# Three id arrays, routing steps and gathers at other places, and T3 kept in PSUM in a chain of attention and two expert layers

## The chip, the cores and the metric

One core of one Trainium2 chip runs one program. The metric is the device time in microseconds (us): the median of 3 runs of the kernel before is 2043.76 us (2043.2 to 2044.96).

## The reference, cut to what matters

```python
# 1. linear attention, B=4 H=8 S=576 D=64, features 2*128
phi = lambda x: concat[exp(p - m), exp(-(p - m))],  p = x @ w_phi, m = max|p|
x = (phi(q) @ (phi(k).T @ v)) / (phi(q) @ sum(phi(k)) + 1e-6)     # -> x[2304, 512]
# 2. soft expert layer, 8 experts, F=1024: every token through every expert
P = exp(x @ w_gate - max); 8 times: rows / sum, columns / sum, * N/E
x = sum_e P[:, e] * (relu(x @ w1[e]) @ w2[e])
# 3. top-1 expert layer: each token through the one expert with the largest cosine
e = argmax(norm(x) @ norm(emb).T / tau);  g = softmax(...)[e]
out = g * (relu(x @ w1[e]) @ w2[e])
```

## The kernel before, in words

All products are made of fp32r parts: each operand is split into a high part (ScalarE cast) and a rest (one subtraction), and three matmuls are summed for one product (L429 to L431).

**First expert layer.** There are 16 half-experts, the groups `n`, and three token batches of 768, so 48 steps `h`. A step is a seven-product Strassen scheme in both layers of the expert: 28 products of six 384-column matmuls. Steps of groups 2 to 14 run through `layers()`; those of groups 0, 1 and 15 run through `p1_group()` and `p2_plain()` with 14 and 16 products. A product is a **tick**. Work beside the products is put on a list by (step, tick): `at_tick()` and `ops_at()` write it, `run_at()` emits it after that product. Each engine then does its instructions in the order in which they were emitted. Ticks of 40 and more in the tables mean the next step.

In `layers()` the hidden halves are B11, B22, T3, T1, T2, B21, T4 in that order. `high()` is a ScalarE cast (L474), `rest()` the subtraction (L477): on GpSimd (POOL in the profile) for B11, B22, T3, T2 and T4, on VectorE (DVE) for T1 and B21. `A.copy(vc, b0)` (L519) empties a PSUM pair that product S4 then writes. T3 is put into an SBUF tile `rc`. `m1c` (L498) is copied into the tile `ra`, which also holds T4's source for its rest.

The last step of each group (`h % NB == NB - 1`) is the **weight-making step**: beside the products it makes the eight split weight pieces of W1 for the next group, and at its end and in the following step those of W2. A piece is a ScalarE cast (L348) and a GpSimd subtraction (L349); four of them first need a GpSimd combination (L354).

**Routing.** Tokens' rows go to DRAM (`x2d`); per tile of 128 tokens an indirect DMA of GpSimd (`route_i`, L960) scatters (token number, gate) pairs into DRAM arrays `ids[k]`, at the slot of the token's expert. There are RB = 6 arrays, one for each tile of a batch of six, and a slot's value is the sum over the arrays. Routing of batches 0 and 6 (tiles) runs in the last two steps (`tail`, by ticks), that of the last batch at the start of `second()`. `route_a` transposes a tile through the PSUM bank "B", of which there is one.

**Second expert layer.** `second()` runs 22 blocks of 128 slots. For each: `load_ids(i)` reads three registers (`value_load`) and issues RB small DMAs on SyncE's queue (L1060); `gather(i)` sums them with a matmul (L1068), VectorE copies token numbers and gates out of PSUM (L1070, L1072), and an indirect DMA of GpSimd fetches the rows (L1074). `tx` transposes and splits them, `p1`, `relu`, `th_`, `p2` are the two layers. `w1_next` and `w2_this` split the weights of the next block's first and this block's second layer on ScalarE and VectorE (L1107, L1108); behind each split a conditional DMA on SyncE (`wcond`, L1079) loads the piece for the block after. Loop order of the kernel before: `load_ids(i+3)`, `p1(i)`, `w1_next(i)`, `relu(i)`, `tx(i+1)`, `w2_this(i)`, `p2(i-1)`, `gather(i+3)`, `th_(i)`. Block 6 is the first whose ids depend on the last batch; `load_ids(6)` stands behind `w2_this(3)`.

Of the kernel before, what the change touches and what calls it, by code (L numbers as in the profile page):

```python
# [23 lines left out]
DM = H * D  # L24
# [5 lines left out]
TH = TB // 2  # L30
NB = NT // TB
TPB = TB // P
RB = 6
NBLK = NT // P + E
REG = NT
NSLOT = 19456
# [8 lines left out]
def build(tc, a, out):  # L45
# [424 lines left out]
    def hraw(tag):  # L470
        return live["h3"].tile([P, 2, TH], F32, tag="r" + tag, name="r" + tag)
# [4 lines left out]
    def rest(nm, src, eng):  # L476
        eng.tensor_tensor(out=hb[nm][:, 1], in0=src, in1=f32(hb[nm][:, 0]), op=ALU.subtract)  # L477
# [6 lines left out]
    def layers(h, n, bi):  # L484
        odd = h % 2
        qx, qz = (0, 3) if odd else (3, 0)

        def tt(out, x, y, op=ALU.subtract):
            V.tensor_tensor(out=out, in0=x, in1=y, op=op)  # L489

        def read(q_, ps, op=ALU.add):
            z = acc(bi)[:, q_]
            V.tensor_tensor(out=z, in0=z, in1=ps, op=op)  # L493

        b0 = pair(qz)
# [24 lines left out]
        b2 = pair(2)  # L520
        yield from twin(b2, 1, "S3", xs["T3"], True)
        tt(b1, b2, vc, ALU.add)
        r22 = hraw("d")
        gate(r22, 1, b1)
        high("B22", r22)
        for i, _ in enumerate(twin(b0, 1, "S4", xs["B22"], False)):
            if i == 0:
                rest("B22", r22, G)
            yield
        gate(b0, 1, b0)  # L530
        t3 = hraw("c")
        tt(t3, r22, b0)
        high("T3", t3)
        tt(b0, b0, r11)
        high("T1", b0)
        for i, _ in enumerate(twin(b2, 1, "A22", xs["T4"], False)):
            if i == 0:
                rest("T3", t3, G)
            yield
        tt(b2, b2, u2c, ALU.add)  # L540
        rest("T1", b0, V)
        tt(r22, r22, b0)
        high("T2", r22)
        gate(b2, 0, b2)
        high("B21", b2)
        X = pair(qx)
        for i, _ in enumerate(twin(X, 2, "A11", hx["B11"], True)):
            if i == 0:
                rest("T2", r22, G)
            yield  # L550
        Y = pair(1)
        yield from twin(Y, 2, "S4", hx["B22"], True)
        read(1, Y, ALU.subtract)
        read(0, X)
        rest("B21", b2, V)
        Z = pair(qz)
        yield from twin(Z, 2, "S1", hx["T1"], True)
        t4 = hraw("a")
        tt(t4, r22, b2)
        high("T4", t4)  # L560
        read(1, Z)
        for i, _ in enumerate(twin(Y, 2, "S3", hx["T3"], False)):
            if i == 0:
                rest("T4", t4, G)
            yield
        read(3, Y)
        yield from twin(X, 2, "S2", hx["T2"], False)
# [303 lines left out]
    def x2c(t0, i, k):  # L871
        return acc(t0 // TPB)[:, 2 * (k // 2) + i // 3, k % 2, (i % 3) * P:(i % 3 + 1) * P]

    def route_a(t0, i):
        r = batch(t0)
        m = TPB // len(r["pieces"])
        row = r["pieces"][i // m][:, i % m]
        ps = psum("B", [P, DM])
        for k in range(KD):
            T.transpose(ps[:, k * P:(k + 1) * P], x2c(t0, i, k), ident)  # L880
        A.activation(out=row, in_=ps, func=AF.Square, accum_out=r["ss"][:, i:i + 1])
        A.copy(row, ps)
# [74 lines left out]

    def route_i(t0, i):
        si = rt[t0]["si"]
        G.indirect_dma_start(out=ids[i], out_offset=bass.IndirectOffsetOnAxis(si[:, i:i + 1], 0), in_=pay[:, t0 + i, :], in_offset=None)  # L960

    meta = c0.tile([1, 3, NBLK], I32, name="meta")
    ebx = c0.tile([1, NBLK + 1], F32, name="ebx")
# [72 lines left out]

    def route_steps(t0, ta, tl, **rest):
        fns = dict(p=route_p, b=route_b, o=route_o, c=route_c, s=route_s, d=route_d, w=route_w)
        ev = [(k, partial(route_l, t0, i)) for i, k in enumerate(tl)] + [(k, partial(route_a, t0, i)) for i, k in enumerate(ta)]
        ev += [(k, partial(fns[nm], t0)) for nm, k in rest.items() if nm != "i"]  # L1040
        return ev + [(k, partial(route_i, t0, i)) for i, k in enumerate(rest["i"])]

# [189 lines left out]
    for h, (n, bi) in enumerate(HS):  # L1232
# [11 lines left out]
        if h % NB == NB - 1 and n + 1 < NGR:  # L1244
            o1, o2 = wops(1, n + 1), wops(2, n + 1, SL1 if n == 0 else SL15 if n == NGR - 2 else {})
            if mixed(n):
                ops_at(h - 1, ((4, "S1r"), (8, "S3r")), o1)
                ops_at(h, ((2, "A11"), (3, "S2r"), (7, "S2"), (8, "A12"), (9, "S4r"), (10, "S1"), (12, "S3"), (14, "S4"), (16, "A22 load")), o1)
            else:
                ops_at(h, ((8, "A11"), (9, "S1r"), (10, "S3r"), (11, "S2r"), (13, "A12"), (14, "S4r"), (16, "S2"), (18, "S1"), (20, "S3"), (22, "S4"), (24, "A22 load")), o1)  # L1250
            if n == 0:
                ops_at(h, ((24, "A11"), (25, "A12"), (26, "A21"), (28, "A22 load")), o2)
            elif n == 1:
                ops_at(h, ((22, "S1r"), (23, "S3r"), (24, "A12"), (26, "A22"), (28, "S3"), (40, "A11"), (41, "S2r"), (42, "S4r"), (44, "S1"), (46, "S4"), (49, "S2 load")), o2)
            elif n == NGR - 2:
                ops_at(h, ((18, "A11"), (24, "A21"), (28, "A12"), (40, "A22 load")), o2)
            else:
                ops_at(h, ((18, "A11"), (20, "S1r"), (21, "S3r"), (25, "S2r"), (40, "A12"), (41, "S4r"), (43, "S1"), (45, "A22"), (46, "S4"), (49, "S3"), (51, "S2 load")), o2)
        if h >= 2 * NB - 1 and h + 1 < NH:
            at_tick(h, 20, partial(load_gate, HS[h + 1][0] // 2, nxt))  # L1260
        if n == NGR - 1:
# [26 lines left out]

    rf = first_blocks()

    tail = route_steps(0, (2, 4, 6, 8, 10, 12), (1, 2, 3, 4, 5, 6), p=13, b=14, o=16, s=18, c=19, w=21, d=23, i=(24, 24, 25, 25, 26, 27))
    tail += route_steps(6, (26, 28, 40, 43, 45, 47), (25, 26, 27, 42, 43, 44), b=46, p=47, o=47, s=48, c=49, w=49, d=49, i=(50, 50, 50, 51, 53, 54))
    tail += [(k, partial(next, rf, None)) for k in (50, 51, 52, 53, 55)] + [(54, partial(load_regs, i)) for i in range(2)]
    tail += [(54, partial(load_raws, 1, range(4))), (55, early_second), (55, start_second)]
    tail += [(56, partial(load_raws, 2, range(4)))]
    tail += [(68 + c, partial(first_w1, 0, (c,))) for c in range(2)]
    tail += [(57 if i < 2 else 69, partial(load_ids, i)) for i in range(4)]
    for i in range(3):
        tail += [(64 + i, partial(route_l, NA, i)), (65 + i, partial(route_a, NA, i))]
    for k, fn in tail:  # L1300
# [51 lines left out]
    def second(i0, i1):  # L1352
# [61 lines left out]
        while i < i1:  # L1414
            early = i + 3 > NEARLY
            if early and i + 3 < i1:
                load_ids(i + 3)
            p1(i)
            if i + 1 < i1:
                w1_next(i, range(4), partial(next, ob, None))  # L1420
            relu(i)
            if i + 1 < i1:
                tx(i + 1)
            w2_this(i, partial(next, ob, None))
            if i + 3 == NEARLY:
                for _ in ob:
                    pass
                load_ids(i + 3)
            if i > i0:
                p2(i - 1, 0)  # L1430
                p2(i - 1, 1)
            if i + 3 < i1:
                gather(i + 3)
            th_(i, 0)
            th_(i, 1)
            i += 1
# [88 lines left out]
```

## Time and profile before

| | |
|---|---|
| median of 3 runs | 2043.76 us |
| profiled execution | 2042.95 us, span of its instructions 2040.9 us |
| TensorE (PE) busy | 1983.3 us, 97% of the span |
| VectorE (DVE), ScalarE (ACT), GpSimd (POOL) busy | 1304.6, 870.3, 1006.6 us |
| mean granted TensorE clock | 0.988 |

The stages on the span: attention to about 230 us, the first expert layer to about 1702 us, the second to the end. The profile's clock and busy shares are near full in all slices but those from about 1690 to 1800 us, the passage from the first expert layer to the second.

### The profile page before, as it was taken

Reading aid. Unit: us, or ns where it says so; the run is one execution under the profiler, and the core shown is the slowest. Engines: PE = TensorE matmul, PEld = TensorE weight load, DVE = VectorE, ACT = ScalarE, POOL = GpSimd, SP = SyncE. Lnnn points to the kernel's source line nnn. Section 1 sums busy time; section 2 is a strip of 40 time slices with the busy share of each in tenths; the row PEclk is TensorE's granted clock in tenths of the full one; section 3 lists DMA queues with packets and bytes.
Section 4 is the critical chain, followed back from the end, with each engine's and each line's share of the span. In section 5 each row is a group of like instructions: output and inputs, shape, how many; then the busy total and the mean of one; then the engine's idle time right before and its main releaser. Section 6 shows DMA issues by size and latency. Waiting matters only on the chain.

```text
span 2040.9 us, 31662 instructions
## 1 busy us (share of the span) xinstructions
PE 1983.3 (97%) x11715; PEld 1900.2 (93%) x11715; DVE 1304.6 (64%) x1852; ACT 870.3 (43%) x1391; POOL 1006.6 (49%) x746
## 2 busy tenths in 40 slices
PE   8999999999999999999999999999999997789998
PEld 8999999999999999999999999999999987678886
DVE  6766556466656655665666566566556453979996
ACT  5566442223332433333243333324333223667775
POOL 1255112666574846657484665748466341322232
PEclk9999999999999999999999999999999997989999
DMA  4345644453735536373553636255362435152761
GB/s 130 109 149 167 227 160 150 141 198 102 250 95 191 163 119 212 97 250 94 192 163 118 218 98 244 94 190 165 117 220 69 157 138 135 22 183 97 286 211 54
DMA packets 119544, 315.16 MB, mean 154 GB/s; under 512 B 11580, under 2 KB 66512, under 8 KB 119386
## 3 DMA queue, kind: packets, MB, share of 16 engines
q1 hardware_dynamic: 115290, 302.57, 44.5%
q0 software_dynamic: 4096, 10.51, 1.6%
q8 instruction: 95, 1.56, 0.3%
q14 instruction: 63, 0.52, 0.1%
HBM read 335.87 MB, written 32.75 MB: 181 GB/s over the span
## 4 chain that ended last, share of the span: by engine, by line
PE 75%; POOL 11%; DVE 5%; issue 4%; DMA 2%; ACT 2%; SPq 1%; POOLq 0%; DVEq 0%; ACTq 0%
PE Q L430 14%; PE Q L429 14%; PE Q L431 14%; PE psD L205 3%; POOL hT L477 3%; PE psD L429 2%; PE psD L430 2%; PE psD L431 2%; POOL w1S L349 2%; PE psA L1135 2%; PE psA L1134 2%; PE psA L1136 2%; PE psA L429 2%; PE psA L431 2%; PE psA L430 2%
## 5 line engine op out<-in xcount | busy, mean ns | idle before, releaser
L493 DVE TENSOR_TENSOR acca<-acca,Q 128x768 f32<-128x768 f32 x182 | 168.8, 952 | 138.9 <-PE Q L431 138.9
L349 POOL TENSOR_TENSOR w1A<-raw,w1A 128x512 fp32r<-128x512 f32 x48 | 62.0, 1293 | 196.7 <-ACT w1A L348 123.6
L429 PE MATMUL Q<-xT,w1S 128*128 128x384 f32 x468 | 156.4, 334 | 0.9 <-ACT ra L498 0.9
L431 PE MATMUL Q<-xT,w1S 128*128 128x384 f32 x468 | 156.4, 334 | 0.0
L430 PE MATMUL Q<-xT,w1S 128*128 128x384 f32 x468 | 156.3, 334 | 0.0
L429 PE MATMUL Q<-hT,w2S 128*128 128x384 f32 x468 | 156.3, 334 | 0.0
L430 PE MATMUL Q<-hT,w2S 128*128 128x384 f32 x468 | 156.3, 334 | 0.0
L431 PE MATMUL Q<-hT,w2S 128*128 128x384 f32 x468 | 156.3, 334 | 0.0
L477 POOL TENSOR_TENSOR hB<-rb,hB 128x768 fp32r<-128x768 f32 x39 | 72.1, 1849 | 137.2 <-ACT hB L474 137.2
L493 DVE TENSOR_TENSOR accb<-accb,Q 128x768 f32<-128x768 f32 x91 | 84.4, 952 | 72.8 <-PE Q L431 72.8
L489 DVE TENSOR_TENSOR Q<-Q,ra 128x768 f32<-128x768 f32 x39 | 37.7, 967 | 124.9 <-PE Q L431 124.9
L1108 DVE TENSOR_TENSOR s1l<-rw,s1h 128x1024 fp32r<-128x1024 f32 x88 | 102.7, 1220 | 16.0 <-ACT s1h L1107 11.8
L498 ACT COPY ra<-Q 128x768 f32<-128x768 f32 x39 | 31.2, 801 | 178.6 <-PE Q L431 156.4
L1108 DVE TENSOR_TENSOR s2l<-rw,s2h 128x1024 fp32r<-128x1024 f32 x76 | 99.0, 1347 | 11.7 <-ACT s2h L1107 9.8
L429 PE MATMUL Q<-xB,w1A 128*128 128x384 f32 x312 | 104.3, 334 | 0.7 <-DVE accb L846 0.7
L431 PE MATMUL Q<-xB,w1A 128*128 128x384 f32 x312 | 104.2, 334 | 0.0
L430 PE MATMUL Q<-xB,w1A 128*128 128x384 f32 x312 | 104.2, 334 | 0.0
L429 PE MATMUL Q<-hB,w2A 128*128 128x384 f32 x312 | 104.2, 334 | 0.0
L430 PE MATMUL Q<-hB,w2A 128*128 128x384 f32 x312 | 104.2, 334 | 0.0
L431 PE MATMUL Q<-hB,w2A 128*128 128x384 f32 x312 | 104.2, 334 | 0.0
L477 POOL TENSOR_TENSOR hT<-ra,hT 128x768 fp32r<-128x768 f32 x39 | 71.9, 1842 | 64.3 <-ACT hT L474 64.3
L477 POOL TENSOR_TENSOR hT<-rd,hT 128x768 fp32r<-128x768 f32 x39 | 72.1, 1850 | 44.5 <-ACT hT L474 44.5
(425 smaller groups left out, 6655.0 us busy)
## 6 DMA issues: line engine op xcount, KB each, us to landing
xT<-xpd SPq DMA_DIRECT2D x120, 768.0 KB
rw<-in_moe_w SPq DMA_DIRECT2D x176, 512.0 KB
xB<-xpd SPq DMA_DIRECT2D x90, 768.0 KB
raw<-in_moe_w SPq DMA_DIRECT2D x34, 512.0 KB
gate<-gd SPq DMA_DIRECT2D x45, 384.0 KB
rx<-in_moe_w SPq DMA_DIRECT2D x30, 512.0 KB
xpd<-xT SPq DMA_DIRECT2D x12, 768.0 KB
xpd<-xB SPq DMA_DIRECT2D x9, 768.0 KB
```

The lines of the kernel that those rows point to most:

```text
L205: T.matmul(ps[:, off:off + w], eq[:, sg, h_, ci * P:(ci + 1) * P], kvz[:, h_, sg, o:o + w], start=(sg == 0), stop=(sg == 1))
L349: eng.tensor_tensor(out=t[:, 1], in0=r(nm), in1=f32(t[:, 0]), op=ALU.subtract)
L429: T.matmul(bank, w[:, 0, j, k, :], x[:, 0, k, :], start=start and k == 0, stop=False, skip_group_check=True)
L430: T.matmul(bank, w[:, 0, j, k, :], x[:, 1, k, :], start=False, stop=False, skip_group_check=True)
L431: T.matmul(bank, w[:, 1, j, k, :], x[:, 0, k, :], start=False, stop=stop and k == 1, skip_group_check=True)
L477: eng.tensor_tensor(out=hb[nm][:, 1], in0=src, in1=f32(hb[nm][:, 0]), op=ALU.subtract)
L489: V.tensor_tensor(out=out, in0=x, in1=y, op=op)
L493: V.tensor_tensor(out=z, in0=z, in1=ps, op=op)
L1108: V.tensor_tensor(out=lo, in0=r, in1=f32(hi), op=ALU.subtract)
L1134: T.matmul(ps[hf], th[:, k, :], wh[:, cs], start=(k == 0), stop=False)
L1135: T.matmul(ps[hf], tl[:, k, :], wh[:, cs], start=False, stop=False)
L1136: T.matmul(ps[hf], th[:, k, :], wl[:, cs], start=False, stop=(k == KD - 1))
```

## The change

There are three id arrays instead of six, so tiles i and i+3 of a batch share one. In the weight-making step T3 is written to the PSUM pair `b1`, its rest is made by VectorE, and both rests (T3, T1) stand ahead of `b2 + u2c`. Weight pieces of that step and the next are emitted at other ticks. Routing of the first two batches is emitted at earlier ticks, with transposes through PSUM bank "D" (two buffers) at ticks below 13. The load of the second layer's W1 is one tick earlier, that of its W2 now behind the first `load_ids`. `gather` is called for block i+2 right behind `p1(i)`, no longer for i+3 behind `p2(i-1)`.

```diff
-RB = 6
+RB = 3
@@ layers()
-        t3 = hraw("c")
+        full = h % NB == NB - 1
+        t3 = b1 if full else hraw("c")
         tt(t3, r22, b0)
         high("T3", t3)
         tt(b0, b0, r11)
         high("T1", b0)
         for i, _ in enumerate(twin(b2, 1, "A22", xs["T4"], False)):
-            if i == 0:
+            if i == 0 and not full:
                 rest("T3", t3, G)
             yield
+        if full:
+            rest("T3", t3, V)
+            rest("T1", b0, V)
         tt(b2, b2, u2c, ALU.add)
-        rest("T1", b0, V)
+        if not full:
+            rest("T1", b0, V)
@@ route_a, route_i, route_steps
-        ps = psum("B", [P, DM])
+        ps = psum(bank, [P, DM])          # bank "D" if k % 40 < 13 else "B"
-        G.indirect_dma_start(out=ids[i], ...
+        G.indirect_dma_start(out=ids[i % RB], ...
@@ weight pieces, mixed groups: W1 in the weight-making step, then W2
-   (2, "A11"), (3, "S2r"), (7, "S2"), (8, "A12"), (9, "S4r"), (10, "S1"), (12, "S3"), (14, "S4"), (16, "A22 load")
+   (2, "A11"), (3, "S2r"), (6, "S2"), (10, "A12"), (11, "S4r"), (12, "S1"), (13, "S3"), (16, "S4"), (17, "A22 load")
-   ..., (43, "S1"), (45, "A22"), (46, "S4"), (49, "S3"), (51, "S2 load")
+   ..., (43, "S1"), (46, "A22"), (47, "S4"), (50, "S3"), (52, "S2 load")
@@ tail
-    tail = route_steps(0, (2, 4, 6, 8, 10, 12), (1, ..., 6), p=13, b=14, o=16, s=18, c=19, w=21, d=23, i=(24, 24, 25, 25, 26, 27))
-    tail += route_steps(6, (26, 28, 40, 43, 45, 47), (25, 26, 27, 42, 43, 44), b=46, p=47, o=47, s=48, c=49, w=49, d=49, i=(50, 50, 50, 51, 53, 54))
-    first_blocks at (50, 51, 52, 53, 55); load_regs 0, 1 at 54
-    load_raws(1) at 54; early_second, start_second at 55; load_raws(2) at 56; load_ids 0, 1 at 57
+    tail = route_steps(0, (1, 2, 4, 6, 8, 10), (1, ..., 6), b=8, o=9, p=11, c=12, s=13, d=14, w=15, i=(16, 16, 18, 19, 20, 21))
+    tail += route_steps(6, (26, 28, 40, 42, 43, 44), (25, 26, 27, 42, 43, 44), b=45, o=45, p=46, s=47, c=47, w=47, d=48, i=(48, 48, 49, 50, 51, 52))
+    first_blocks at (49, 50, 51, 52, 54); load_regs 0, 1 at 53
+    load_raws(1) at 53; early_second, start_second at 54; load_raws(2) at 57; load_ids 0, 1 at 56
@@ second()
             p1(i)
+            if i + 2 < i1 and i + 2 not in xg:
+                gather(i + 2)
...
                 p2(i - 1, 1)
-            if i + 3 < i1:
-                gather(i + 3)
             th_(i, 0)
```

(The lines on ticks of `first_blocks` and the loads are put in words; load_ids 2 and 3 stay at tick 69.)

## Rows read from the trace of the kernel before

**Rows 1.** Stages: length, busy PE, PEld, DVE, ACT, POOL (instructions), clock, DMA share, GB/s
```profile
485.00:1570.00 1085.00, 1078.46 (x6138) 1062.32 (x6138) 670.44 (x734) 390.03 (x541) 676.33 (x454) 1.00 0.49 159
...
1700.00:1720.00 20.00, 10.60 (x52) 10.24 (x51) 4.50 (x8) 6.64 (x13) 1.95 (x2) 0.62 0.46 169
...
1800.00:2026.00 226.00, 225.85 (x1109) 186.12 (x1108) 204.09 (x217) 171.53 (x222) 63.24 (x50) 1.00 0.52 181
```
**Rows 2.** Waits of PE, whole span: us in total, times, longest
```profile
PE psB L1068 <- DMA idr<-ids: 18.5, 3, 9.1
...
PE Q L430 <- POOL hT L477: 3.3, 12, 0.3
...
PE Q L430 <- POOL hB L477: 2.6, 13, 0.2
```
**Rows 3.** Timeline of PE, one weight-making step: start, us, instruction, [idle before <-releaser]
```profile
578.41 0.34 PE L431 MATMUL Q<-xT,w1S 128*128 128x384 f32 x1
578.78 0.45 PE L429 MATMUL Q<-xB,w1S 128*128 128x384 f32 x1
...
585.15 0.34 PE L429 MATMUL Q<-hB,w2S 128*128 128x384 f32 x1
585.67 0.44 PE L430 MATMUL Q<-hB,w2S 128*128 128x384 f32 x1 [0.18 <-POOL hB L477]
...
598.72 0.45 PE L430 MATMUL Q<-hT,w2A 128*128 128x384 f32 x1 [0.26 <-POOL hT L477]
```
**Rows 4.** Timeline of POOL, the same step (rest of T3, a piece, rest of T4)
```profile
586.85 1.84 POOL L477 TENSOR_TENSOR hT<-rc,hT 128x768 fp32r<-128x768 f32 x1
588.65 1.30 POOL L349 TENSOR_TENSOR w1S<-raw,w1S 128x512 fp32r<-128x512 f32 x1
...
596.83 1.84 POOL L477 TENSOR_TENSOR hT<-ra,hT 128x768 fp32r<-128x768 f32 x1
```
**Rows 5.** Timelines of ACT and DVE, the same step
```profile
577.42 0.61 ACT L348 CAST w1A<-raw 128x512 fp32r<-128x512 f32 x1
577.94 0.79 ACT L519 COPY rc<-Q 128x768 f32<-128x768 f32 x1
...
587.08 0.84 ACT L474 CAST hT<-rd 128x768 fp32r<-128x768 f32 x1 [1.37 <-DVE rd L489]
...
585.23 0.96 DVE L477 TENSOR_TENSOR hT<-Q,hT 128x768 fp32r<-128x768 f32 x1 [0.34 <-ACT hT L474]
```
**Rows 6.** Timeline of SyncE's DMA queue, passage to the second layer: start, length, count
```profile
1687.14 5.57 SPq L1079 DMA_DIRECT2D rw<-in_moe_w  x8
1697.67 12.18 SPq L1060 DMA_DIRECT2D idr<-ids  x12
...
1713.74 16.36 SPq L1060 DMA_DIRECT2D idr<-ids  x24
...
1788.05 7.16 SPq L1060 DMA_DIRECT2D idr<-ids  x12
```
**Rows 7.** Timeline of PE: first gather, first matmuls of p1(0) and p1(4)
```profile
1707.25 0.98 PE L1068 MATMUL psB<-ones,idr 6*128 6x1 f32 x4 [5.37 <-DMA idr<-ids]
...
1725.34 0.80 PE L1134 MATMUL psA<-s1h,xth 128*128 128x512 f32 x1
...
1794.37 0.78 PE L1134 MATMUL psA<-s1h,xth 128*128 128x512 f32 x1
```
**Rows 8.** The tile ids: issue of a scatter to its landing
```profile
DMA to landing us min/median/max: 3.8/5.7/6.6
```
**Rows 9.** Timelines of DVE and POOL, one block of the second layer
```profile
1862.41 4.63 DVE L1108 TENSOR_TENSOR s1l<-rw,s1h 128x1024 fp32r<-128x1024 f32 x4
...
1868.34 5.39 DVE L1108 TENSOR_TENSOR s2l<-rw,s2h 128x1024 fp32r<-128x1024 f32 x4 [0.26 <-ACT s2h L1107]
...
1868.20 1.04 POOL L1105 CAST s2h<-rw 128x1024 fp32r<-128x1024 f32 x1 [5.36 <-issue]
```
**Rows 10.** Timeline of SyncE's queue at the start: the id arrays are filled
```profile
6.06 3.36 SPq L282 DMA_DIRECT2D ids<-sent  x6
```

More of the change, by code (lines that the diff above doesn't have):

```diff
@@ L872, in x2c, with route_a @@
         return acc(t0 // TPB)[:, 2 * (k // 2) + i // 3, k % 2, (i % 3) * P:(i % 3 + 1) * P]
-    def route_a(t0, i):
+    def route_a(t0, i, bank="B"):
         r = batch(t0)
@@ L959, in route_i @@
         si = rt[t0]["si"]
-        G.indirect_dma_start(out=ids[i], out_offset=bass.IndirectOffsetOnAxis(si[:, i:i + 1], 0), in_=pay[:, t0 + i, :], in_offset=None)
+        G.indirect_dma_start(out=ids[i % RB], out_offset=bass.IndirectOffsetOnAxis(si[:, i:i + 1], 0), in_=pay[:, t0 + i, :], in_offset=None)
     meta = c0.tile([1, 3, NBLK], I32, name="meta")
@@ L1038, in route_steps @@
         fns = dict(p=route_p, b=route_b, o=route_o, c=route_c, s=route_s, d=route_d, w=route_w)
-        ev = [(k, partial(route_l, t0, i)) for i, k in enumerate(tl)] + [(k, partial(route_a, t0, i)) for i, k in enumerate(ta)]
+        ev = [(k, partial(route_l, t0, i)) for i, k in enumerate(tl)] + [(k, partial(route_a, t0, i, "D" if k % 40 < 13 else "B")) for i, k in enumerate(ta)]
         ev += [(k, partial(fns[nm], t0)) for nm, k in rest.items() if nm != "i"]
@@ L1247, in build @@
                 ops_at(h - 1, ((4, "S1r"), (8, "S3r")), o1)
-                ops_at(h, ((2, "A11"), (3, "S2r"), (7, "S2"), (8, "A12"), (9, "S4r"), (10, "S1"), (12, "S3"), (14, "S4"), (16, "A22 load")), o1)
+                ops_at(h, ((2, "A11"), (3, "S2r"), (6, "S2"), (10, "A12"), (11, "S4r"), (12, "S1"), (13, "S3"), (16, "S4"), (17, "A22 load")), o1)
             else:
@@ L1257, in build @@
             else:
-                ops_at(h, ((18, "A11"), (20, "S1r"), (21, "S3r"), (25, "S2r"), (40, "A12"), (41, "S4r"), (43, "S1"), (45, "A22"), (46, "S4"), (49, "S3"), (51, "S2 load")), o2)
+                ops_at(h, ((18, "A11"), (20, "S1r"), (21, "S3r"), (25, "S2r"), (40, "A12"), (41, "S4r"), (43, "S1"), (46, "A22"), (47, "S4"), (50, "S3"), (52, "S2 load")), o2)
         if h >= 2 * NB - 1 and h + 1 < NH:
@@ L1289, in build @@
     rf = first_blocks()
-    tail = route_steps(0, (2, 4, 6, 8, 10, 12), (1, 2, 3, 4, 5, 6), p=13, b=14, o=16, s=18, c=19, w=21, d=23, i=(24, 24, 25, 25, 26, 27))
-    tail += route_steps(6, (26, 28, 40, 43, 45, 47), (25, 26, 27, 42, 43, 44), b=46, p=47, o=47, s=48, c=49, w=49, d=49, i=(50, 50, 50, 51, 53, 54))
-    tail += [(k, partial(next, rf, None)) for k in (50, 51, 52, 53, 55)] + [(54, partial(load_regs, i)) for i in range(2)]
-    tail += [(54, partial(load_raws, 1, range(4))), (55, early_second), (55, start_second)]
-    tail += [(56, partial(load_raws, 2, range(4)))]
+    tail = route_steps(0, (1, 2, 4, 6, 8, 10), (1, 2, 3, 4, 5, 6), b=8, o=9, p=11, c=12, s=13, d=14, w=15, i=(16, 16, 18, 19, 20, 21))
+    tail += route_steps(6, (26, 28, 40, 42, 43, 44), (25, 26, 27, 42, 43, 44), b=45, o=45, p=46, s=47, c=47, w=47, d=48, i=(48, 48, 49, 50, 51, 52))
+    tail += [(k, partial(next, rf, None)) for k in (49, 50, 51, 52, 54)] + [(53, partial(load_regs, i)) for i in range(2)]
+    tail += [(53, partial(load_raws, 1, range(4))), (54, early_second), (54, start_second)]
+    tail += [(57, partial(load_raws, 2, range(4)))]
     tail += [(68 + c, partial(first_w1, 0, (c,))) for c in range(2)]
-    tail += [(57 if i < 2 else 69, partial(load_ids, i)) for i in range(4)]
+    tail += [(56 if i < 2 else 69, partial(load_ids, i)) for i in range(4)]
     for i in range(3):
```

## The prediction

> **What bounds the kernel now.** I read the stage table first. From 485 to 1570 us TensorE issues 6138 matmuls in 1085 us, 0.177 each with all stops in it, and is busy 99.4% [rows 1]: only the stops can go. From 1800 to 2026 it is busy 225.85 of 226 us: there nothing can be gained, but VectorE, busy 204 of 226, is near to being the bound. Between them the stage 1700 to 1720 has 10.6 us of TensorE in 20, at a granted clock of 0.62. The second view, the waits of TensorE over the span, names what the table shows: 18.5 us in three waits for the ids of a gather, the longest 9.1, and two small families in the group loop, 12 waits for POOL's rest of T4 (3.3 us) and 13 for POOL's rest of B22 (2.6 us) [rows 2]. Third, timelines of one weight-making step and of SyncE's queue in the passage to the second layer, to see what made those late.
>
> **The group loop, T3 and the pieces.** In the step of rows 3 TensorE stops three times. At 578.78 product S4 starts 0.37 us behind the matmul ahead of it, where 0.17 is the pace, and runs 0.45 instead of 0.34: 0.31 us lost, because ScalarE made the cast of W1's A12 (577.42, 0.61 us) ahead of the copy that empties S4's bank (577.94 to 578.73) [rows 3, 5]. At 585.67 it stands 0.35 + 0.10 = 0.45 us for the rest of B22, and before 598.72 0.26 us and a restart of 0.1 for that of T4. The first kind comes once more in the next step, for a piece of W2. Twelve or thirteen of each: 12.5 * (0.31 + 0.45 + 0.36 + 0.31) = 18 us is the most there is.
>
> With A12 at tick 10 it is cast behind the copy, which then ends at 577.5 + 0.8 = 578.3, ahead of S4: 0.31 goes, and in the next step too (S3 from 49 to 50). POOL now runs: rest of B11 from 577.6 (its cast ends where that of 577.42 began), A12 and S4r, rest of B22: 577.6 + 1.85 + 2 * 1.3 + 1.85 = 583.9 [rows 4], 1.7 us ahead of need: that stop goes. But T4 does not profit as much. S1 and S3 follow to 586.5; then POOL waits for T2, since S4 moved behind it (tick 16). T2's source comes later, because the rest of T3 now stands ahead of it on VectorE (0.96 us, as the rest of T1 from PSUM); it fills the idle 0.34 us ahead of T1's rest, and S4's stop of 0.3 us is gone: T2's cast ends at 587.08 + 0.84 + 0.96 - 0.34 - 0.3 = 588.2 instead of 587.9 [rows 5]. From there POOL does the rest of T2, five pieces and combinations (S4, A22, W2's A11, S1r, S3r) and the rest of T4: 2 * 1.85 + 5 * 1.3 = 10.2, end at 598.4 to 598.5, against 598.67 now [rows 4]. POOL's 1.84 us saved on T3 are thus spent waiting, and T4 comes only some 0.2 to 0.3 us earlier. So T4 takes most of the time that the other two stops free: per group I take 0.3 us from this step (between 0 and 0.76) and 0.3 from the next, 0.6 * 12.5 = 7.5 us. Bounds: 2.5 (only half of the next step's stops go) and 18. The pair `b1` is wanted again by W2's S4 at 585.15 - 0.3 = 584.85 [rows 3]; T3's rest takes the slot of the 0.96 us that end ahead of T1's idle time, at 585.23 - 0.34 = 584.9, less 0.2 to 0.3 [rows 5]. So this new use costs 0 to 0.1 us, which T4's stop would take up.
>
> **The start.** Filling the arrays takes 3.36 us of SyncE's queue for six transfers [rows 10], ahead of the loads of q and k that the first products wait for; three fewer are 1.7 us, and their bytes stop sharing the engines. I take 2.5 us; bounds 0 (other loads late anyway) and 3.4.
>
> **The last two steps.** Routing of six tiles comes up to eight ticks earlier in step 46 and one or two in step 47. VectorE's work there is the same, in another order; two transposes that waited about 0.5 us for bank B get bank D. I take 0, bounds -1.5 and +3. Tiles i and i+3 now write one array. If GpSimd has to let the first scatter land before it issues the second, it stands: three scatters go out 1.3 us apart, each lands in 5.7 us [rows 8], so the fourth waits some 2 us (it is emitted one or two products later) and the last lands about 14 us after the first. The first goes out about 3 us earlier than now. Queued behind the waiting scatters on POOL is one rest of T1's tile, used by TensorE 8 us later; that cover is some 4 us thick. The page DMA: Bandwidth & Descriptors of the Trainium skill, section Two DMAs through the same engine are not ordered, says that the issuing engine has to wait for the semaphore of the first transfer; no row of the kernel before shows this wait, as its six arrays had none so close.
>
> **The ids of blocks 0 and 1.** Now eight weight loads go out from 1687.14 and the 12 id transfers only from 1697.67, one per us until 1709.85: they stand behind the big transfers [rows 6]. After the change four weight loads come first, then six id transfers, then the other four; with the registers read about 1 us earlier the ids land about 1696, before the last product at 1701.9 (1707.25 less 5.37) [rows 7]. VectorE then still splits two weight pieces (2 * 1.2) ahead of the first token copy, so the second gather's matmul comes at about 1705.4, not 1712.3. The three routed tiles that follow go at ScalarE's pace, 2.5 us each. So p1(0) starts at about 1716 instead of 1725.34: 9 us. Bounds: 4, if the ids are as late as the lone first wait (5.37), and 13, if the clock stays at its full level. The ids of blocks 2 to 5 take 12 transfers less than the 24 of 1713.74; SyncE's reading of registers in front of each set stays, so 3 us of 16.4 go.
>
> **The ids of block 6.** The wait of 9.1 us lies in iteration 3, where `gather(6)` comes right behind `load_ids(6)`, whose transfers start at 1788.05 behind conditional loads that wait for VectorE's splits [rows 2, 6]. Now `gather(5)` stands there and `gather(6)` behind p1(4). What is late next: VectorE does the copies of `gather(5)` only once p1(3) is done, which I estimate to put the splits of block 3's second layer, and `load_ids(6)` behind them, 2.5 us later: transfers from 1790.5, landed about 1793.5 (three transfers and some 2 us). TensorE ends p2(2) at 1794.37 - 2.5 (gather and transposes) - 9.1 = 1782.8 [rows 2, 7]; 1.5 us for gather and transposes, about 5.5 for p1(4): 1789.7. So 9.1 becomes about 4, with a restart at half clock as now, and a little more goes since p1(4) itself is done: 6 us gained, bounds 0 and 9.
>
> **The 17 blocks after it.** VectorE now meets the token copies right behind p1(i); the splits of the next block (4.63 us), which ran beside p1(i), start behind them. A block has 64 matmuls, so 1109 are 17.3 blocks of 13.0 us, with 204.09 / 17.3 = 11.8 us of VectorE [rows 1]. From the end of p1(i) a chain runs over the gather's matmuls (0.98 us at most [rows 7]) and all of VectorE's work: 4.63 + 5.39 [rows 9] and 1.8 of smaller operations, 12.8. Its last result is wanted by p2(i), behind p1(i+1), a gather and a transposition: 13.0 + 1. So about 1.2 us are to spare. The gather now runs on GpSimd beside those splits. Beside a GpSimd cast of 1.04 us four splits took 5.39, without one 4.63 us, 0.76 more [rows 9]. The page SBUF — State Buffer, section Who interferes with whom, calls the port that both share an exclusive lock, which the trace agrees with; by that rule the gather costs VectorE up to its 1 us a block, which would leave next to nothing of that. I take 3 us in all, for the blocks at which an expert changes and its eight pieces are asked for 2 to 4 us later. Bounds 0 and 34 (2 us in each).
>
> **Sum.** -7.5 - 2.5 + 0 - 9 - 6 + 3 = -22 us. The profiled execution took 2042.95 us (its span 2040.9), 0.8 under the median shown: 2042.95 - 22 = 2021 there, and 2021.5 us as a median.
>
> **Rivals.** *A, the id waits move.* The scatters' landing holds the ids of block 0 and those of block 6 are as late as now. For it: SyncE serves all in one order, and three arrays make scatters wait. Against it: eight big transfers become four in front. Then only the loop, the start and some 2 us go: 2043.8 - 12 = 2032. *B, all stops of the group loop go,* because T4 comes early after all: 18 instead of 7.5: 2011. For it: 1.84 us less work on POOL. Against it: the wait for T2. *C, slower: the second layer becomes bound by VectorE.* The place is the token copy behind p1(i): from the point at which VectorE's work in a block passes 13.0 us, each of 17 blocks is longer by the excess. With 0.76 from the gather it is 12.6; weights that come 2.4 us too late in each would make it 15.0, 2 us a block: 34 instead of the 3 above, 2021.5 + 31 = 2052. Against it: 12.6 is under 13.0, and weights are loaded only where the expert changes. *D, no change:* the loop gains nothing and the passage gives back what it saves, 2044.
>
> **How the numbers follow.** Forecast 0.55, A 0.18, B 0.16, C 0.07, D 0.04. What can't be told from no change is 0.2%, 4 us. Faster by more: 0.55 + 0.18 + 0.16 = 0.89; slower 0.07; same 0.04. The range reaches from below B (its 2011 with a passage better by 7) to beyond A (its 2032 with no gain at the start), 2004 to 2035; C, D and the ends of A and B are left out. The likeliest case alone is 2013 to 2029.
>
> **What would show it.** Right, if the stops at S4 and for B22 are gone from the loop and one stop for T4's rest of 0.5 to 1 us stays, POOL standing idle ahead of T2; if p1(0) starts about 9 us earlier, counted from the last product, and one wait of 3 to 5 us for ids stays, at the gather of block 6; and if the blocks from 7 on take 13.0 us. Wrong, if TensorE waits in the second layer's blocks for splits, or at the first gather for ids.

## The result, and the profile after

The changed kernel took 2022.05 us in the median of 4 runs (2020.45 to 2023.27), the kernel before 2043.66 beside it: ratio 0.9893, 95% interval 0.9876 to 0.991. The forecast was 2021.5. The profiled execution took 2022.27 us with a span of 2020.5. The total came out as forecast partly because errors cancelled: the last two steps took 5.2 us more than forecast, blocks 0 to 2 of the second layer 4.5 us less.

The table below follows TensorE from landmark to landmark in the two traces (start of the matmul named, us; the gain is the sum up to that point).

| landmark | before | after | gain | stretch | predicted |
|---|---|---|---|---|---|
| first group-loop product | 419.20 | 418.82 | 0.4 | start −0.4 | −2.5 |
| last group-loop product | 1577.85 | 1568.72 | 9.1 | loop −8.75 | −7.5 |
| last product ahead of the second layer | 1701.55 | 1697.63 | 3.9 | last two steps **+5.2** | 0 |
| p1(0) | 1725.34 | 1714.27 | 11.1 | ids of blocks 0, 1 −7.2 | −9 |
| p1(3) | 1764.99 | 1749.42 | 15.6 | blocks 0 to 2 **−4.5** | none |
| p1(5) | 1808.53 | 1787.36 | 21.2 | ids of block 6 −5.6 | −6 |
| p1(20) | 2002.93 | 1982.36 | 20.6 | later blocks +0.6 | +3 |

The stage table after, with the same columns as [rows 1], for the loop, the passage and the later blocks:

```profile
485.00:1560.00 1075.00, 1070.13 (x6130) 1061.13 (x6130) 679.63 (x746) 386.47 (x539) 653.91 (x440) 1.00 0.49 160
1690.00:1710.00 20.00, 17.31 (x102) 16.86 (x101) 5.76 (x11) 10.17 (x20) 1.94 (x2) 0.78 0.50 165
1780.00:2005.00 225.00, 225.00 (x1097) 185.15 (x1097) 201.86 (x219) 170.17 (x220) 75.67 (x51) 0.99 0.53 185
```

The loop has 0.1754 us a matmul instead of 0.177. TensorE's waits after (us in total, times, longest):

```profile
PE psA L1140 <- DVE xtl L1125: 5.0, 1, 5.0
PE Q L429 <- DVE rd L489: 4.1, 13, 0.3
PE psB L1073 <- DMA idr<-ids: 3.0, 1, 3.0
PE psB L1073 <- DVE gt L1077: 2.7, 1, 2.7
...
PE psA L429 <- DVE ci L976: 1.5, 1, 1.5
...
PE psB L931 <- DVE oh L921: 1.3, 1, 1.3
```

Beside [rows 2], the 18.5 us of id waits are 3.0, and the waits for GpSimd's rests of T4 and B22 have left the list; a row with 13 times 0.3 us for VectorE's `rd` is new. The longest wait now, 5.0 us in p1(3), isn't: the kernel before has it too, with 4.3 us. It is for VectorE's split of block 3's rows, which stands behind the last batch's slot tables and weight splits. T4's stop has no row in the list any more, but it is still there in the timeline: a gap without a named releaser. So I also took every start of a 384-column matmul more than 0.25 us behind the start of the one ahead, less the pace of 0.1735. Before: at S4 7.9 us, for B22 6.1, for T4 6.6, 21.9 in all. After: B22's are gone and S4's but for one, T4 has 4.1, and 13 stops ahead of W2's S1 have 6.2; 11.9 in all. TensorE's timeline after, at this new stop and at T4's:

```profile
585.71 0.34 PE L431 MATMUL Q<-hB,w2S 128*128 128x384 f32 x1
586.37 0.41 PE L429 MATMUL Q<-hT,w2S 128*128 128x384 f32 x1 [0.32 <-DVE rd L489]
...
596.85 0.34 PE L429 MATMUL Q<-hT,w2A 128*128 128x384 f32 x1
597.27 0.44 PE L430 MATMUL Q<-hT,w2A 128*128 128x384 f32 x1
```

VectorE and then GpSimd in the same step of the kernel after:

```profile
582.62 1.88 DVE L477 TENSOR_TENSOR hT<-Q,hT 128x768 fp32r<-128x768 f32 x2
584.41 0.95 DVE L489 TENSOR_TENSOR Q<-Q,u2c 128x768 f32<-128x768 f32 x1
585.28 0.94 DVE L489 TENSOR_TENSOR rd<-rd,Q 128x768 f32<-128x768 f32 x1
```
```profile
587.17 1.86 POOL L477 TENSOR_TENSOR hT<-rd,hT 128x768 fp32r<-128x768 f32 x1 [1.90 <-ACT hT L474]
...
595.37 1.85 POOL L477 TENSOR_TENSOR hT<-ra,hT 128x768 fp32r<-128x768 f32 x1
```

`r22 - b0` (the instruction at 585.28) reads the pair of banks that S1's product of W2 is to overwrite. T3's rest, one instruction more ahead of it, makes it end at 586.22, when the product was due at 585.9. GpSimd stands idle 1.90 us ahead of T2's rest, as predicted, and T4's rest, at 595.37, still comes last.

In the passage the ids now leave ahead of the second four weight loads. SyncE's queue, as [rows 6], and TensorE's gathers, as [rows 7]:

```profile
1681.48 3.62 SPq L1084 DMA_DIRECT2D rw<-in_moe_w  x4
1685.35 3.61 SPq L1065 DMA_DIRECT2D idr<-ids  x6
1690.04 3.29 SPq L1084 DMA_DIRECT2D rw<-in_moe_w  x4
...
1703.32 11.04 SPq L1065 DMA_DIRECT2D idr<-ids  x12
...
1716.61 57.28 SPq L1084 DMA_DIRECT2D rw<-in_moe_w  x32
```
```profile
1697.89 0.63 PE L1073 MATMUL psB<-ones,idr 3*128 3x1 f32 x4
1701.21 0.96 PE L1073 MATMUL psB<-ones,idr 3*128 3x1 f32 x4 [2.69 <-DVE gt L1077]
...
1778.48 0.60 PE L1073 MATMUL psB<-ones,idr 3*128 3x1 f32 x4 [3.03 <-DMA idr<-ids]
```

The first gather waits for nothing, the second for VectorE's token copy, and 3.03 us remain at block 6's gather.

The last two steps, which lost 5.2 us, show it on VectorE and GpSimd. First VectorE, then GpSimd (its first row is the first batch's), then TensorE in step 47:

```profile
1663.54 0.56 DVE L445 SCALAR_TENSOR_TENSOR graw<-psA,gate 128x384 f32<-128x384 f32 x1
1667.12 0.17 DVE L937 TENSOR_SCALAR ss<-ss 128x6 f32<-128x6 f32 x1 [3.02 <-POOL ss L901]
```
```profile
1639.66 0.96 POOL L965 DMA_INDIRECT ids<-pay,si  x1 [3.48 <-DMA ids<-pay,si]
...
1664.77 1.01 POOL L462 TENSOR_TENSOR hT<-graw,hT 128x384 fp32r<-128x384 f32 x1 [3.47 <-ACT hT L461]
1665.73 1.36 POOL L901 TENSOR_TENSOR ss<-ss,ones 128x6 f32<-128x6 f32 x1
...
1677.84 0.97 POOL L965 DMA_INDIRECT ids<-pay,si  x1 [1.78 <-DMA ids<-pay,si]
1679.53 0.96 POOL L965 DMA_INDIRECT ids<-pay,si  x1 [0.72 <-DMA ids<-pay,si]
```
```profile
1661.90 0.18 PE L931 MATMUL psB<-oh,tri 128*128 128x48 bf16 x1 [1.33 <-DVE oh L921]
1662.88 0.18 PE L932 MATMUL psB<-ohc,onesb 128*128 128x48 bf16 x1 [0.80 <-DVE ohc L923]
```

The second batch's power (L901) needs GpSimd behind a rest of the layer (L462) that stood 3.47 us for its cast; VectorE's normalisation stands 3.02 us for the power, with the layer's sums queued behind it. GpSimd's wait for a scatter to land, 3.48, 1.78 and 0.72 us, is there as predicted, and TensorE has no wait for it.

TensorE's stops of more than 0.15 us in these steps sum to 7.7 us, against 5.2 before. The rest of the loss goes in part with the granted clock: it is at its lower level (0.50) for 6.8 us of these steps, before for 3.4.

### The profile page after: what moved, and what is told of

It is laid out like the page before. It is cut to its first block, busy times and chain, and to the rows that moved or that the text cites. A ratio compares the mean times of both kernels' runs of the same rounds, so it can differ in the third digit from the quotient of the medians.

```text
span 2020.5 us, 31417 instructions
## 1 busy us (share of the span) xinstructions
PE 1978.7 (98%) x11715; PEld 1901.4 (94%) x11715; DVE 1309.5 (65%) x1865; ACT 869.2 (43%) x1391; POOL 995.1 (49%) x733
## 4 chain that ended last, share of the span: by engine, by line
PE 76%; POOL 8%; DVE 6%; issue 5%; DMA 2%; ACT 2%; SPq 1%; POOLq 0%; DVEq 0%; ACTq 0%
PE Q L430 15%; PE Q L429 14%; PE Q L431 14%; PE psD L205 3%; PE psD L429 2%; PE psD L430 2%; PE psD L431 2%; POOL w1S L349 2%; PE psA L429 2%; PE psA L1140 2%; PE psA L431 2%; PE psA L430 2%; PE psA L1141 2%; POOL hB L477 2%; PE psA L1139 2%
## 5 line engine op out<-in xcount | busy, mean ns | idle before, releaser
L1113 DVE TENSOR_TENSOR s1l<-rw,s1h 128x1024 fp32r<-128x1024 f32 x88 | 112.4, 1332 | 9.6 <-ACT s1h L1112 7.4
L1079 POOL DMA_INDIRECT xgs<-x2d,idt x22 | 35.6, 1619 | 126.3 <-DVE gt L1077 126.0
```

What stands on the lines that cost most here:

```text
L1113: V.tensor_tensor(out=lo, in0=r, in1=f32(hi), op=ALU.subtract)
```

## The experiments

The twelve kernels are edits of the changed kernel, each timed against the kernel before. Lengths are from their traces: *loop* from the first to the last matmul of the group loop, *last two* from there to the last product, *passage* from there to p1(0), *0 to 5* from p1(0) to p1(5). The attention's last row of matmuls starts between 223.07 and 227.79 us in these traces, in no order with the number of arrays (224.28 and 226.24 with six). In the kernel after and the five whose edits leave the loop alone its length is 1149.56 to 1149.90, so 1 us of it can be told from none. *Last two* scatters more, and with the clock: in the nine kernels that leave the routing's ticks as changed it is 127.68 without a stretch at the lower level there (old ticks), 127.64 to 127.89 with 3.4 us of it (six arrays, old gather, T4 on VectorE) and 128.74 to 128.93 with 6.8 us (the other five).

| kernel | loop | last two | passage | 0 to 5 | median us | ratio to before, 95% |
|---|---|---|---|---|---|---|
| before | 1158.65 | 123.70 | 23.79 | 83.19 | 2043.66 | 1 |
| after | 1149.90 | 128.91 | 16.64 | 73.09 | 2022.05 | 0.9876–0.991 |
| T3 in SBUF | 1147.93 | 128.90 | 16.69 | 72.92 | 2019.72 | 0.9871–0.9901 |
| old ticks | 1153.69 | 127.68 | 16.69 | 72.94 | 2025.82 | 0.9905–0.9932 |
| six arrays | 1149.79 | 127.89 | 15.63 | 81.84 | 2030.69 | 0.9925–0.9952 |
| old routing | 1149.71 | 124.79 | 15.89 | 72.31 | 2017.61 | 0.9862–0.9892 |
| old gather | 1149.56 | 127.64 | 16.30 | 78.05 | 2025.9 | 0.9898–0.9925 |
| weights first | 1149.90 | 128.86 | 16.70 | 72.94 | 2022.92 | 0.9875–0.991 |
| T2 first | 1147.11 | 128.74 | 16.68 | 72.87 | 2018.09 | 0.985–0.988 |
| early power | 1149.65 | 124.96 | 16.68 | 73.03 | 2017.08 | 0.9848–0.9879 |
| T4 on VectorE | 1145.41 | 127.82 | 16.68 | 73.28 | 2017.96 | 0.9854–0.9884 |
| reads first | 1176.48 | 128.93 | 16.69 | 72.97 | 2047.91 | 1.0004–1.0022 |
| reads first, early power | 1176.61 | 124.97 | 16.67 | 73.14 | 2044.35 | 0.9989–1.0007 |
| `r22 - b0` first, early power | 1143.13 | 126.19 | 16.57 | 73.24 | 2013.46 | 0.983–0.9857 |

**T3 in SBUF.**
```diff
-        full = h % NB == NB - 1
+        full = False
```


> T3 goes back to SBUF and its rest to GpSimd in the weight-making step; all else stays as changed. Theory (GpSimd only waits for T2's source in the time that T3's rest would take): no loss. The 13 stops of S1 behind VectorE's T2 operation (6.2 us with their restarts) go, the 12 stops for T4's rest grow from 0.2 to about 0.7 us: 2020 to 2024 us, within 2.5 us of the changed kernel's 2022. Rival (taking T3 off GpSimd is what made the group loop 8.8 us shorter): 2028 to 2031 us, with stops of more than 1 us at T4.

The stops ahead of S1 are gone, and those for T4 take 10.4 us instead of 4.1. TensorE's waits:

```profile
PE Q L430 <- POOL hT L477: 6.9, 12, 0.6
```

The theory was right. Beside the moved pieces, keeping T3 in PSUM brings nothing: without it the loop is 2.0 us shorter.

**Old ticks of the weight pieces.**
```diff
-ops_at(h, (... (6, "S2"), (10, "A12"), (11, "S4r"), (12, "S1"), (13, "S3"), (16, "S4"), (17, "A22 load")), o1)
+ops_at(h, (... (7, "S2"), (8, "A12"), (9, "S4r"), (10, "S1"), (12, "S3"), (14, "S4"), (16, "A22 load")), o1)
-... (46, "A22"), (47, "S4"), (50, "S3"), (52, "S2 load")), o2)
+... (45, "A22"), (46, "S4"), (49, "S3"), (51, "S2 load")), o2)
```


> The weight pieces go back to their old ticks; T3 stays in PSUM. Theory (the ticks remove the stops at S4 and for B22; T3 in PSUM removes none of these): 25 stops at S4 of 0.3 us and 13 for B22 of 0.45 come back, 13.6 us, and the stops at S1 and T4 (10.3 us) mostly go: 2024 to 2028 us. Rival (the ticks are the whole gain of the loop): 2030 to 2032 us.

S4's stops (7.9 us) and B22's (6.1) are back as in the kernel before, T4's and S1's are gone. With T3 in PSUM alone the loop gains 5.0 us (1158.65 to 1153.69), with the new ticks alone 10.7, with both 8.75: the two parts don't add up, they hinder each other.

**Six arrays.**
```diff
-RB = 3
+RB = 6
```


> Six id arrays again, all else as changed; no scatter then waits for another. Theory (SyncE's queue is shorter with three arrays: its 12 id transfers of blocks 2 to 5 took 11.0 us, the 24 before took 16.4): the loads for block 1 come about 5 us later, p1(2) starts 4 us later, the ids of block 6 about 1 us later: 2026 to 2030 us. Rival (the order of the loads and the place of the gather make the gain, the number of arrays does not): 2021 to 2023 us; if the scatters' waits cost anything, below 2021.

p1(1) comes as in the kernel after (1721.36 against 1721.74), p1(2) 6.2 us later and p1(5) 8.9: the theory's place, at somewhat more than its price (2030.69 us against 2026 to 2030). SyncE's queue shows why:

```profile
1704.88 16.55 SPq L1065 DMA_DIRECT2D idr<-ids  x24
...
1723.69 56.24 SPq L1084 DMA_DIRECT2D rw<-in_moe_w  x32
```

The weight loads of the next blocks stand behind the ids of blocks 2 to 5; with three arrays they start at 1716.61. ScalarE's cast of a weight piece in p1(1) stands 6.4 us for its load with six arrays, 4.1 in the kernel before, and not at all in the kernel after. The first gathers wait for no ids with six arrays either.

**Old routing ticks** (the first batch's `route_steps(0, ...)` is as in the kernel before too; the calls behind the routing are a tick later than in the kernel after, with that kernel's order of loads).
```diff
-route_steps(6, ..., b=45, o=45, p=46, s=47, c=47, w=47, d=48, i=(48, 48, 49, 50, 51, 52))
+route_steps(6, ..., b=46, p=47, o=47, s=48, c=49, w=49, d=49, i=(50, 50, 50, 51, 53, 54))
```


> Routing of the first two batches at its old ticks, the loads in the new order one tick later. Theory (the earlier routing made the last two steps 5.2 us longer, since VectorE stood 3.0 us behind GpSimd's power of the norms and TensorE behind both): the last product comes 3 to 5 us earlier counted from the end of the group loop; the ids of blocks 0 and 1 come about 3 us later and still land before it: 2017 to 2020 us. Rival (the ids need the earlier routing): a stop of 3 us or more at the first gather and 2022 to 2026 us.

The last two steps are 4.1 us shorter, and no gather waits for the first ids.

**Old gather.**
```diff
             p1(i)
-            if i + 2 < i1 and i + 2 not in xg:
-                gather(i + 2)
...
                 p2(i - 1, 1)
+            if i + 3 < i1:
+                gather(i + 3)
```


> The gather of the loop goes back to block i+3 behind p2(i-1); all else as changed. Theory (the new place lets p1(4) run during the wait for the ids of block 6): a stop of 7 to 9 us comes back at that gather ahead of p1(4), where the changed kernel stands 3.0 us behind p1(4); p1(5) starts 5 to 6.5 us later: 2026.5 to 2029 us. Rival (three arrays alone shorten that wait, the place is nothing): 2021 to 2023.5 us.

The wait for ids is back, at the lower end of what the theory expected, and the time is a little below its range. TensorE's waits:

```profile
PE psB L1073 <- DMA idr<-ids: 7.0, 1, 7.0
```

**Weights first.**
```diff
-    tail += [(57, partial(load_raws, 2, range(4)))]
+    tail += [(55, partial(load_raws, 2, range(4)))]
```


> The four loads of the second layer's W2 go back ahead of the ids of blocks 0 and 1, as in the kernel before; all else as changed. Theory of the prediction (these loads in front are what made the ids late): the id transfers start about 1692 instead of 1685 us and go out one per us; a stop of 1 to 4 us for ids comes back at the first two gathers: 2023 to 2026 us. Rival (with half the transfers and an earlier start the ids still land before the last product at 1697.6, or under VectorE's two weight splits that the second gather waits for anyway): 2021 to 2023 us, no wait for ids there.

The rival was right. All eight weight loads go ahead of the ids again, and the first gather still waits for none. SyncE's queue:

```profile
1683.10 6.54 SPq L1084 DMA_DIRECT2D rw<-in_moe_w  x8
1689.89 6.28 SPq L1065 DMA_DIRECT2D idr<-ids  x6
```

**T2 first.**
```diff
             rest("T3", t3, V)
+            tt(r22, r22, b0)
+            high("T2", r22)
             rest("T1", b0, V)
```


> In the weight-making step VectorE makes T2's source (r22 - b0) right behind T3's rest, ahead of T1's rest and of b2 + u2c; all else as changed. Theory (S1 waits for this operation, since it reads the pair that S1 writes, and GpSimd waits for T2's cast ahead of the pieces that make T4 late): both remaining kinds of stops go, 10.3 us with restarts: 2011 to 2014 us, no stop of TensorE over 0.25 us in the loop. Rival (GpSimd has too much work up to T4 whatever the order): only S1's stops go and T4's grow, 2017 to 2022 us.

S1's stop went, but a stop of 0.26 us with a slow restart came one product later, at W2's S3 (4.5 us in all). The timeline names no releaser for it; S3 is added to a bank that VectorE reads first, and that read, the first of two, began at 591.23 with the product due at 591.97. T4's stop stayed as it was (4.2 us). The loop gains 2.8 us: the time is in the rival's range, but not by the rival's account, in which T4's stops grow.

**Early power.**
```diff
-b=45, o=45, p=46, s=47, c=47, w=47, d=48
+b=45, o=45, p=45, s=47, c=48, w=47, d=48
```


> In the last step the power of the norms on GpSimd is emitted one tick earlier (45), ahead of the rest of T1's tile, and the rank matmuls one tick later (48); all else as changed. Theory (VectorE stood 3.0 us for that power, and TensorE 2.1 us for the one-hot sums and 1.5 us for VectorE): 2.5 to 4.5 us go: 2017.5 to 2019.5 us. Rival (VectorE's routing work as a whole, wherever its waits are, makes the last steps longer): 2021 to 2023 us.

The last two steps take 124.96 us instead of 128.91, and VectorE's wait of 3.0 us for the power is gone. Not all of the 4.0 us is the queue's: the clock stays at its full level in these steps here, in the kernel after it does not. Against old ticks (127.68), where it stays there too, 2.7 us go, and TensorE's stops of more than 0.15 us fall from 8.9 to 6.1 us. So the two moves undo half to three quarters of the loss; they were made together, so what the power does alone isn't shown.

**T4's rest on VectorE.**
```diff
-                rest("T4", t4, G)
+                rest("T4", t4, V if full else G)
```


> Of the changed kernel one instruction of each of the 13 weight-making steps goes to another engine: the rest of T4 is made by VectorE instead of GpSimd, where it stood behind three weight pieces (ready at 591.42 us, begun at 595.37, done at 597.22; the product on T4 stops at 596.85). Theory (T4's stop is GpSimd's queue): VectorE is idle for 0.61 and 1.12 us in that stretch, so the 0.95 us instruction costs it nothing; T4's 12 stops (4.1 us with the slow restart) go, the 13 stops of 0.3 us ahead of S1's product stay; the group loop ends 4 us earlier, 2017 to 2019 us against 2022. Rival (VectorE is the fuller engine of the step): the next read of a bank begins later and a stop of 0.2 us or more takes T4's place; 2020 to 2023.

As the theory said, T4's stops are gone, S1's are as they were (6.1 us), the loop is 4.5 us shorter. VectorE, then GpSimd at the new place:

```profile
593.65 0.96 DVE L477 TENSOR_TENSOR hT<-ra,hT 128x768 fp32r<-128x768 f32 x1
594.53 1.81 DVE L493 TENSOR_TENSOR accb<-accb,Q 128x768 f32<-128x768 f32 x2
```
```profile
592.45 1.31 POOL L349 TENSOR_TENSOR w1A<-raw,w1A 128x512 fp32r<-128x512 f32 x1
593.70 2.06 POOL L349 TENSOR_TENSOR w2A<-rx,w2A 128x512 fp32r<-128x512 f32 x1
```

**Reads first.**
```diff
             rest("T3", t3, V)
+            tt(r22, r22, b0)
+            high("T2", r22)
             rest("T1", b0, V)
         tt(b2, b2, u2c, ALU.add)
...
         read(0, X)
+        if full:
+            gate(b2, 0, b2)
+            high("B21", b2)
         rest("B21", b2, V)
```


> As the kernel with T4's rest on VectorE, and VectorE's order in the weight-making step is T3's rest, r22 - b0, T1's rest, b2 + u2c, then the two sums that read the banks of the products on B22 and B11, and only then gate(b2); the kernel that only put r22 - b0 ahead of T1's rest stopped 0.26 us ahead of the product on T3 in each step, where these sums ended at 592.2. Theory (all three stops of the step are the order of VectorE's and GpSimd's queues, not their load): stops of 6.2 and 4.1 us fall to under 2 us together; the group loop takes 1140 to 1142 us instead of 1149.9; 2012 to 2015 us. Rival (VectorE's thirteen instructions in a row from the split of r22 on are too many for the step in any order): another stop of 0.2 to 0.3 us appears, at the product on B21 or on T4, and the loop takes 1145 us or more; 2017 or more.

30 us slower than the kernel with T4's rest alone moved: the theory fell, and the rival's point of 2017 is passed by far more than its stops of 0.3 us would give. TensorE in one weight-making step, then VectorE and GpSimd in another:

```profile
689.78 0.44 PE L429 MATMUL Q<-xB,w1A 128*128 128x384 f32 x1 [1.98 <-DVE acca L493]
...
691.21 0.52 PE L429 MATMUL Q<-xB,w1A 128*128 128x384 f32 x1
```
```profile
593.54 0.96 DVE L477 TENSOR_TENSOR hB<-Q,hB 128x768 fp32r<-128x768 f32 x1 [0.87 <-ACT hB L474]
...
596.26 2.07 DVE L477 TENSOR_TENSOR hT<-ra,hT 128x768 fp32r<-128x768 f32 x1
598.25 2.67 DVE L493 TENSOR_TENSOR accb<-accb,Q 128x768 f32<-128x768 f32 x3
```
```profile
596.22 1.29 POOL L354 TENSOR_TENSOR rx<-rx,rx 128x512 f32<-128x512 f32 x1
597.59 1.86 POOL L354 TENSOR_TENSOR rx<-ws,rx 128x512 f32<-128x512 f32 x1
```

VectorE stood 0.87 us for ScalarE's copy of B21; T4's rest then met a GpSimd instruction and took 2.07 us instead of 0.96; the three sums behind it, which free banks, came too late for the next step's first product. That is 12 stops of 2.15 us (25.8); in the 13th step T4's rest meets no GpSimd instruction at its start and takes 0.96 us. Behind seven of the stops TensorE then runs slowly: in the step shown it starts nine matmuls 0.32 us apart after standing for 1.98 us, and the granted clock is 0.60 from 690 to 693, most of that stretch at the lower of its levels (1.2 GHz).

**Reads first, early power.** The two edits together.

> As the kernel with the sums ahead of gate(b2), and in the second batch's routing GpSimd's power (the square root of the sums of squares) is issued a tick earlier and the class scores a tick later, which alone gave 5 us in the last two steps. Theory (the two are in different stretches and both sums hold): 5 us less than that kernel, 2007 to 2011 us. Rival (the last product's end only moves to where the ids are waited for): under 2 us less than that kernel.

The 4.0 us in the last two steps come again, and the loss of the loop too. The theory's half on the power holds in the main (3.6 us in the medians; the 5 us that it starts from was a difference of medians, too); its total of 2007 to 2011 fell with the kernel that it built on.

**`r22 - b0` first, early power.**
```diff
             rest("T1", b0, V)
+            tt(r22, r22, b0)
+            high("T2", r22)
         tt(b2, b2, u2c, ALU.add)
...
         read(1, Y, ALU.subtract)
+        if full:
+            gate(b2, 0, b2)
+            high("B21", b2)
         read(0, X)
...
         high("T4", t4)
+        if full:
+            rest("B21", b2, V)
```
(and T4's rest on VectorE, and `p=45`, `c=48`)

> The kernel with T4's rest on VectorE (2018.0 us; its 13 stops of 0.3 us ahead of S1's product remain, 6.1 us), with two more edits: in the weight-making step VectorE does r22 - b0 ahead of b2 + u2c, gate(b2) between the two sums that free the banks, and B21's rest after T4's subtraction, so that it stands for ScalarE's copy of B21 nowhere; and GpSimd's power is issued a tick earlier in the second batch's routing. Theory (the remaining stop is VectorE's order and not its load; the kernel with both sums ahead of gate(b2) lost 28 us because two waits on ScalarE pushed the third sum past the next step's product): r22 - b0 ends at 585.4 instead of 586.2 in the step's time, the product on T1 is due at 585.9; 6 us less in the loop and 5 us less in the last two steps, 2006 to 2009 us. Rival (the queue is full and the stop moves on, to the product on T3 or the next step's first): only the 5 us of the power, 2012 to 2014; with a stop like the 2.2 us one, over 2030.

2013.46 us: faster than both kernels, but by the rival's account. The stop ahead of S1 is gone, and one of 0.16 us with a slow restart stands ahead of the next step's first product (5.0 us in all). TensorE, then VectorE:

```profile
596.75 0.34 PE L431 MATMUL Q<-hB,w2A 128*128 128x384 f32 x1
597.25 0.44 PE L429 MATMUL Q<-xB,w1A 128*128 128x384 f32 x1 [0.16 <-DVE accb L493]
```
```profile
594.16 1.31 DVE L477 TENSOR_TENSOR hT<-ra,hT 128x768 fp32r<-128x768 f32 x1
595.39 2.69 DVE L493 TENSOR_TENSOR accb<-accb,Q 128x768 f32<-128x768 f32 x3
```

From 582.5 to 598.1 VectorE works there without a gap, so the theory (order and not load) fell, and each order that was tried only chose which product pays. How much of this stop is load isn't shown: in all 13 steps T4's rest takes 1.29 to 1.31 us beside GpSimd instead of 0.96, and that 0.35 us is about as long as the stop. No run kept the two apart. The loop is 2.3 us shorter than with T4's rest alone, and the last two steps gave 2.7 us against the kernel after, not 4, with 3.4 us of them at the lower clock level. T3 in SBUF together with T4's rest on VectorE, which would take an instruction from it, wasn't tried.

## Why the prediction was right, and where it was not

**The group loop: size right, place wrong.** S4's and B22's stops went as worked out, and GpSimd idles ahead of T2. The step that failed is "this new use costs 0 to 0.1 us": it looked at the pair that T3 stays in (`b1`), not at what T3's rest pushes back on VectorE. There `r22 - b0` had to free S1's pair, 6.2 us a run. That stop may in turn have given T4's rest the time that it lacked, as T4's stops fell to 4.1 us (0.34 each, where the prediction's sign was 0.5 to 1); no run shows one without the other. With T3 in SBUF, where S1 doesn't stop, the predicted mechanism is seen by itself, but smaller: T4's stops grow from 6.6 to 10.4 us, 3.8 of the 14.0 that S4 and B22 free, not most of them. The saving of 0.3 us per step was thus right as a sum only. And "18 us is the most there is" took 0.36 us for T4's stop; with the slow restart it measures 0.55, and the three kinds 20.6 us.

**The start: mis-sized, nothing seen.** 0.4 us instead of 2.5, and the traces scatter by 4.7 us there. If fewer transfers gain anything, these runs can't show it.

**The last two steps: the step that failed outright.** I wrote that "VectorE's work there is the same, in another order" and took 0, at most +3; it cost 5.2. What I left out is that the routing's power runs on GpSimd, in a queue where the entry ahead of it is a layer's rest standing for its cast. The early power with the later rank matmuls gives 4.0 us of it back (2.7 at an equal clock), the old routing 4.1. The 1.3 us that are left with the early power are not accounted for. The scatters that wait for landing, my candidate for a loss here, cost nothing that TensorE shows: GpSimd stood 3.48, 1.78 and 0.72 us.

The page DMA: Bandwidth & Descriptors of the Trainium skill, section Two DMAs through the same engine are not ordered, asks for this wait between dependent transfers; the trace after has it in these three rows. The kernel with six arrays has none in any batch.

**The ids of blocks 0 and 1: size near, the reason half right.** 7.2 us instead of 9. The second gather's matmul comes 3.6 us behind the last product, as forecast (3.5). From there to p1(0) it is 13.1 us in the kernel before and after; the forecast took 10.6 there, and that term was mis-sized. That the ids "stand behind the big transfers" is so in the kernel before: SyncE waits for weight loads to land,

```profile
SPq L1060 <- DMA rw<-in_moe_w: 14.1, 10, 4.7
```

and 11.7 us of it are in front of the first eight id transfers; the 4.7 us are what lies between the eighth weight load (1692.7) and the first ids (1697.67) [rows 6]. In the kernel after the first six ids wait 1.1 us, with weights first 3.6. But the order of the loads alone is not what did it: with all eight weight loads first no gather waits for ids, nor with six arrays in the new order, nor with the old routing ticks. Each of these keeps some of the parts, and in all of them the ids leave SyncE between 9 and 12 us ahead of the last product, in the kernel before 3.9. Why the first weight loads took longer to land in the kernel before was not isolated.

**Blocks 0 to 2: a gain that the text saw and did not count.** It says that 3 of 16.4 us of id transfers go. That their end is the start of 32 weight loads was not followed: from p1(1) to p1(2) it is 15.4 us instead of 19.5, and 22.0 with six arrays.

**The ids of block 6: right.** 5.6 us against 6, the remaining wait 3.03 against "about 4". With the old gather 5.0 us come back between p1(0) and p1(5). **The later blocks: hardly a loss.** From p1(6) to p1(20) it is 182.0 us after 181.4, since one gather more falls into it; a block with a gather takes 13.0 us in both. In 182 us of that stretch VectorE is busy 164.73, before 168.39. The cost of the gather to VectorE, put at 0.76 to 1 us a block, is nothing there: 22 splits beside a gather's indirect DMA alone took 1.22 us each, those beside nothing 1.21 to 1.22, and only splits beside a GpSimd cast up to 2.08. The +3 was not needed, and rival C has no support. A fell with the waits, B with S1's stop.

## What to carry to other kernels

When an instruction goes to the front of an in-order engine, list what moves back behind it and which bank or buffer each of those frees; the price is there, not at the tile that was moved. Where three engines share a step that is nearly full, test the parts alone and together: here two gains of 5.0 and 10.7 us made 8.75. A total that agrees with its forecast proves no term of it; a landmark table tests each. And before a few microseconds of a stretch are put down to a queue, compare the granted clock in it.

## What the runs showed that I had not expected

Of a VectorE subtraction with both sources in SBUF and a GpSimd instruction, the one that starts second is slowed: GpSimd's 1.30 us became 2.06 beside VectorE's 0.96, and VectorE's 0.96 became 2.07 behind a GpSimd instruction that started 0.04 us earlier. The page SBUF — State Buffer of the Trainium skill, section Who interferes with whom, calls the port that the two share an exclusive lock, and both pairs agree with it to 0.15 us (what is left of the first and the whole of the second would be 2.21 us each).

A stop of 2 us in the loop can cost more than itself: after one of 1.98 us nine matmuls started 0.32 us apart instead of 0.1735, 1.3 us more. Seven of the twelve stops had such a stretch at the lower clock level behind them, five of the same length had none.
